# A first quarter of w_in on the plain queue, and batch 0's attention in another order

## The chip, the cores and the metric

The kernel runs on one core of a Trainium2 chip, in one launch. The metric is the device time of that launch in microseconds (us), taken as the median of several runs; the page and the answers of the trace come from one profiled execution. Engines are named as in the profile: PE (TensorE), PEld (its weight loads), DVE (VectorE), ACT (ScalarE), POOL (GpSimd), SP (SyncE). A q behind a name means the engine's instruction queue. DMAs are issued by SP, ACT or POOL.

## The reference

Two stages, each of which takes the whole of the one before. q, k and v are [8 batches, 8 heads, 576 positions, 64] in float32.

```python
scores = scale * q @ k.T                       # per batch and head
rel = pos[:, None] - pos[None, :]
mask = (rel >= 0) & (rel < 128)                # causal, window of 128
scores = where(mask, scores - slopes[h] * abs(rel), -1e9)
attn = softmax(scores)
x = (attn @ v) as [4608 tokens, 512]
h = x @ w_in                                   # w_in [512, 2048]
out = (h * clip(h + 3, 0, 6) / 6) @ w_out      # w_out [2048, 512]
```

## The kernel before

**Tiles.** Attention goes by pairs of heads: four pairs per batch, 32 in all, numbered g = 4 * batch + pair. In a pair the scores fall into diagonal blocks (four of 128x128 per head, bank scd) and blocks off the diagonal (sco). The second stage goes by nine groups of 512 tokens. An "up" unit (moe_up, L462) makes 128 of the 2048 hidden columns for 512 tokens: four matmuls (L451, one for each 128-row slice of x and w_in, called k slice here), one activation on ACT (L470) and one product on DVE (L471) into gbuf. A "down" unit (moe_down, L488) runs four matmuls (L501) of a quarter of w_out for 128 tokens; after four of them the tokens are written out. For the first token group there are 16 up units: 0 to 3 need the first quarter of w_in, 4 to 7 the second, and so on.

**Order.** All engines run a written order (manual_schedule, L718): each engine takes its instructions as the program issues them and waits only for the data and buffers of each. fill(n) (L523) issues the next n units of one list; an up unit is skipped, and the list stands still, as long as the batches that it needs are not done. ORDER (L513) is the list's mixture of ups (U) and downs (D) for each pair of token groups.

**Batch 0** (first_batch, L558). q and k of a pair come as float32 runs (load_run, four transfers on SP's queue, four on ACT's). prepare (L204) casts them to bf16, transposes (L211) turns them on PE, 18 small transposes for q and 18 for k, and copies them out into qTb and kTb. The ALiBi bias and the mask of batch 0 are added on PE: tables_diag (L266) and tables_off (L299) write a table into the bank before the scores are added, so that one exponential covers both heads; where diag_tabled (L263) is false, each head has its own exponential with a bias, and POOL masks the result with a select (L354). The results of batch 0 lie in the still empty w_out_sb. The order is a chain of rounds: transposes of pair g + 1 stand on PE behind the diagonal scores of pair g. When all four pairs have their exponentials, v's five pieces are cast, and attend (L399) multiplies with v for a whole pair in one double bank of ps_sc; DVE divides by the sums (L412, L413). back (L421) transposes the result on PE into the single bank ps_o, and ACT copies it into xT (L438), which is the x of the second stage; for the last pair ACT and DVE copy a part each (L434, L435).

**Weights.** w_in comes in four quarters of 512 columns (load_w_in, L165), float32 in memory and cast to bf16 by the transfer itself, which POOL issues. The first is issued behind a cast of v, the second (second_w_in, L175) behind a write to w_out_sb that waits for pair 1's values, the third and fourth behind the casts of batch 1's q and k. Those come as eight double loads (load_double, L96) on SP's queue, behind batch 0's v (load_tokens, L108); prepare_double (L223) casts them on POOL, wide_double (L248) turns nine 128x128 blocks on PE and copies them out in one piece. Batch 1's v follows on SP's queue.

**Into the second stage.** up_begin (L455) starts a unit with the k slices that are already there: unit 0 with three slices before pair 3 is back, unit 1 with three behind it. fill(1), the turn of batch 1's k, and fill(2) follow; then second_batch (L620) runs batch 1's scores with three units to each pair.

PSUM has eight banks: ps_sc two double ones (scores, attend, wide_double), ps_h two, ps_av and ps_o one each.

Of the kernel before, what the change touches and what calls it, by code (L numbers as in the profile page):

```python
# [18 lines left out]
def kernel(  # L19
# [88 lines left out]
    def load_tokens(b, nm):  # L108
        t = tokens(b, nm)
        for j in range(NQ):  # L110
            n = min(128, S - j * 128)
            nc.sync.dma_start(out=t[:n, j, :, :],
                              in_=src_of[nm][b, :, ds(j * 128, n), :].rearrange("h p d -> p h d"))
# [90 lines left out]
    def prepare(g, copies):  # L204
        for nm, copy in zip("qk", copies):
# [5 lines left out]
    def transposes(g, copies):  # L211
        b, hp = divmod(g, NP)
        for nm, dst, copy in (("q", qTb[b % 2], copies[0]), ("k", kTb[b % 2], copies[1])):
            src = st.pop((g, nm))
            tp = ps_h.tile([128, RT, RP], BF16, tag="h", name="tp", padded_shape=[128, 16, 64])
            for t in range(RT):
                for e in range(2):
                    r = slice(e * D, (e + 1) * D)
                    nc.tensor.transpose(tp[r, t, :], src[r, ts(t, D)], ident[r, r])
            copy(out=dst[:, hp, :, :].rearrange("p j c -> p (j c)")[:, 0:S].rearrange(  # L220
                "p (a t) -> p a t", t=RT), in_=tp.rearrange("p t a -> p a t"))
# [11 lines left out]

    BANKS = {"h": ps_h, "av": ps_av, "o": ps_o}
# [28 lines left out]
    def diag_tabled(g):  # L263
        return g < NP
# [109 lines left out]
    def av_matmuls(g, qts, where):  # L374
# [3 lines left out]
        for qt in qts:  # L378
            for e in range(2):
# [14 lines left out]
    def values(g, qts):  # L394
# [3 lines left out]
        if qts[0] == 0:  # L398
# [5 lines left out]
            in1=rc[:, 0:nq, :, :].to_broadcast([128, nq, 2, D]), op=ALU.mult)  # L404

# [107 lines left out]
    ORDER = [("UUDUDUUDUD", "UUDUDUDUD", "UDUDUDD", "UUDDDD"),  # L513
# [44 lines left out]
    def first_batch():  # L558
        prepare(0, (V, A))
# [27 lines left out]
        load_w_in(0)  # L587
        cast_v(0, 2, V)
        cast_v(0, 3, V)
        cast_v(0, 4, P)  # L590
# [24 lines left out]
        done[0] = NP  # L615
        fill(1)
        wide_double(1, 0, "k", A)
        fill(2)
# [99 lines left out]
    with tc.manual_schedule(engines=every):  # L718
# [7 lines left out]
        load_tokens(0, "v")  # L726
        constants()
# [38 lines left out]
```

## Time and profile before

| | us |
|---|---|
| median of 3 runs | 323.79 (322.96 to 326.55) |
| profiled execution, whole | 323.38 |
| its span, first to last instruction | 321.7 |
| busy in the span: PE | 308.1 (96%) |
| ACT | 195.1 (61%) |
| DVE | 172.7 (54%) |
| POOL | 140.7 (44%) |

The granted TensorE clock is 1.00 over the span. The DMA engines move 51.90 MB, 161 GB/s on average; over the first two thirds of the span their mean busy share is 0.9 or more, later 0.1 to 0.3. HBM is read for 36.70 MB.

A row of the profile names the line of the kernel, the engine, the operation, the tile that is written and those that are read, with partitions x elements; then how many there are, how long they are busy in all or on average, and how long the engine stood idle before them and for whom. In the rows in order of time the first two columns are the start from the span's beginning and the length, in us. In the table by stretches each engine has its busy time and, in brackets, its number of instructions; PEclk is the granted clock, the last two columns are the mean busy share of the 16 DMA engines (over 1 where packets of several queues overlap) and the GB/s moved. The busy time of PE is modelled from the starts of its matmuls, so a full PE there need not be at its peak.

### The profile page before, as it was taken

Reading aid. Unit: us, or ns where it says so; the run is one execution under the profiler, and the core shown is the slowest. Engines: PE = TensorE matmul, PEld = TensorE weight load, DVE = VectorE, ACT = ScalarE, POOL = GpSimd, SP = SyncE. Lnnn points to the kernel's source line nnn. Section 1 sums busy time; section 2 is a strip of 40 time slices with the busy share of each in tenths; the row PEclk is TensorE's granted clock in tenths of the full one; section 3 lists DMA queues with packets and bytes.
Section 4 is the critical chain, followed back from the end, with each engine's and each line's share of the span. In section 5 each row is a group of like instructions: output and inputs, shape, how many; then the busy total and the mean of one; then the engine's idle time right before and its main releaser. Section 6 shows DMA issues by size and latency. Waiting matters only on the chain.

```text
span 321.7 us, 7010 instructions
## 1 busy us (share of the span) xinstructions
PE 308.1 (96%) x2699; PEld 166.7 (52%) x2738; DVE 172.7 (54%) x338; ACT 195.1 (61%) x334; POOL 140.7 (44%) x249
## 2 busy tenths in 40 slices
PE   6879999999999999999999999999999999999996
PEld 5465465555555455455677644554554444444443
DVE  6657675554356555555555556555655455455510
ACT  4748976877777766666676657666764344244401
POOL 8456592683494767356745664563331000000000
PEclk9999999999999999999999999999999999999999
DMA  7999999899999999999999999932112200000112
GB/s 277 202 319 225 272 255 208 223 235 204 220 223 184 220 198 201 200 223 205 186 191 191 229 176 201 211 108 86 23 53 64 76 34 35 33 33 33 67 52 79
DMA packets 131425, 51.90 MB, mean 161 GB/s; under 512 B 118976, under 2 KB 123328, under 8 KB 131392
## 3 DMA queue, kind: packets, MB, share of 16 engines
q1 hardware_dynamic: 126160, 45.36, 67.0%
q0 software_dynamic: 4224, 4.19, 8.3%
q10 hardware_dynamic: 1008, 1.90, 1.6%
q8 instruction: 21, 0.34, 0.5%
q14 instruction: 12, 0.10, 0.1%
HBM read 36.70 MB, written 9.44 MB: 143 GB/s over the span
## 4 chain that ended last, share of the span: by engine, by line
PE 82%; DMA 5%; ACT 4%; POOL 4%; issue 2%; DVE 2%; SPq 1%; POOLq 0%
PE ops L501 35%; PE hps L451 35%; DMA ldbuf<-in_q_dram 3%; PE scd L296 2%; DMA qTb<-tbuf 2%; PE av L391 2%; PE av L383 2%; ACT r L470 2%; PE sco L328 1%; PE ops L482 1%; ACT kTb L244 1%; PE tp L254 1%; POOL tbuf L194 1%; ACT gbuf L351 1%; SPq L98 1%
## 5 line engine op out<-in xcount | busy, mean ns | idle before, releaser
L471 DVE SCALAR_TENSOR_TENSOR gbuf<-r,hps 128x512 bf16<-128x512 f32 x144 | 98.7, 687 | 102.5 <-ACT r L470 100.2
L470 ACT ACTIVATE r<-hps,bias 128x512 f32<-128x512 f32 x144 | 98.9, 689 | 89.5 <-PE hps L451 88.2
L451 PE MATMUL hps<-xT,w_in_sb 128*128 128x512 bf16 (+1 forms) x621 | 142.7, 358 | 2.3 <-DMA w_in_sb<-in_moe_w_in_dram 0.9
L501 PE MATMUL ops<-w_out_sb,gbuf 128*128 128x512 bf16 x540 | 134.2, 380 | 2.3 <-issue 1.7
L451 PEld LDWEIGHTS <-w_in_sb 128*128 128x128 bf16 x640 | 58.8, 98 | 54.8 <-DMA w_in_sb<-in_moe_w_in_dram 1.3
L501 PEld LDWEIGHTS <-gbuf 128*128 128x128 bf16 x560 | 52.2, 98 | 57.2
L354 POOL TENSOR_SCALAR_AFFINE_SELECT pd<-pd 128x512 bf16<-128x512 bf16 x48 | 29.6, 631 | 34.5 <-ACT pd L351 34.4
L364 POOL TENSOR_SCALAR_AFFINE_SELECT po<-po 128x512 bf16<-128x512 bf16 x48 | 30.1, 633 | 32.7 <-ACT po L361 32.6
L351 ACT ACTIVATE pd<-scd,bias_d 128x512 bf16<-128x512 f32 x48 | 31.6, 685 | 5.0 <-PE scd L296 3.6
L194 POOL CAST tbuf<-ldbuf 128x512 bf16<-128x512 f32 (+1 forms) x45 | 25.5, 611 | 18.7 <-DMA qTb<-tbuf 9.8
L510 DVE COPY osb<-ops 128x512 f32<-128x512 f32 x33 | 22.7, 687 | 20.3 <-PE ops L501 20.3
L361 ACT ACTIVATE po<-sco,bias_o 128x512 bf16<-128x512 f32 x48 | 33.1, 689 | 0.0
L402 DVE TENSOR_TENSOR avs<-av,rc 128x384 bf16<-128x384 f32 (+1 forms) x48 | 23.6, 491 | 1.6
L391 PEld LDWEIGHTS <-pd 128*128 128x128 bf16 x192 | 14.4, 97 | 8.3 <-issue 0.5
L383 PE MATMUL av<-vbuf,po 128*128 128x65 bf16 x192 | 18.1, 193 | 0.1
L391 PE MATMUL av<-vbuf,pd 128*128 128x65 bf16 x192 | 17.5, 194 | 0.3 <-ACT kTb L244 0.3
L383 PEld LDWEIGHTS <-po 128*128 128x128 bf16 x192 | 14.4, 98 | 3.1 <-DVE avs L402 0.5
L187 POOL CAST vbuf<-ldbuf 128x1024 bf16<-128x1024 f32 x14 | 14.3, 1040 | 3.2 <-DMA ldbuf<-in_v_dram 3.2
L367 ACT ACTIVATE p4buf<-sco,bias_d 128x64 bf16<-128x64 f32 x48 | 15.5, 324 | 0.0
L227 POOL CAST pr<-ldbuf 128x576 bf16<-128x576 f32 x20 | 12.8, 669 | 4.4 <-DMA ldbuf<-in_k_dram 3.4
L296 PE MATMUL scd<-qTb,kTb 64*128 64x128 bf16 x256 | 12.7, 219 | 1.8 <-DVE kTb L220 1.1
L296 PEld LDWEIGHTS <-kTb 64*128 64x128 bf16 x256 | 7.2, 94 | 13.5 <-issue 9.7
(96 smaller groups left out, 215.0 us busy)
## 6 DMA issues: line engine op xcount, KB each, us to landing
out_dram<-osb SPq DMA_DIRECT2D x33, 256.0 KB, 2.4
ldbuf<-in_v_dram SPq DMA_DIRECT2D x32, 256.0 KB, 5.3
ldbuf<-in_q_dram SPq DMA_DIRECT2D x20, 256.0 KB, 5.1
ldbuf<-in_k_dram SPq DMA_DIRECT2D x16, 256.0 KB, 4.6
ldbuf<-in_q_dram SPq DMA_DIRECT2D x12, 288.0 KB, 6.4
ldbuf<-in_k_dram SPq DMA_DIRECT2D x12, 288.0 KB, 6.4
w_in_sb<-in_moe_w_in_dram POOLq DMA_DIRECT2D x4, 512.0 KB, 9.2
w_out_sb<-in_moe_w_out_dram POOLq DMA_DIRECT2D x4, 512.0 KB, 11.1
```

The source lines that it names most:

```text
L194: nc.gpsimd.tensor_copy(out=tbuf[:m, :, j, :], in_=s[:m, j, :, :].rearrange("p (i e) d -> p i (e d)", e=2))
L296: nc.tensor.matmul(scd[:, e, ts(j, 128)], lhsT=kT[r, j, :], rhs=qT[r, j, :], start=first, stop=first or j == 3)
L351: nc.scalar.activation(out=pd[:, e, :, :].rearrange("p j c -> p (j c)"), in_=sc[:, e, :], func=ACT.Exp, bias=bias_d[:, h:h + 1], scale=scale)
L354: nc.gpsimd.affine_select(out=pd[:, e, :, :], in_=pd[:, e, :, :], pattern=[[0, 4], [1, 128]], channel_multiplier=-1, base=0, compare_op=AL ...
L361: nc.scalar.activation(out=po[:, e, :, :].rearrange("p j c -> p (j c)"), in_=sc[:, e, :], func=ACT.Exp, bias=bias_o[:, h:h + 1], scale=scale)
L364: nc.gpsimd.affine_select(out=po[:, e, :, :], in_=po[:, e, :, :], pattern=[[0, 4], [-1, 128]], channel_multiplier=1, base=-1, compare_op=A ...
L383: nc.tensor.matmul(out_av, lhsT=po[:, e, qt % 4, :], rhs=vb[:, qt - 1, h, :], start=True, stop=False)
L391: nc.tensor.matmul(out_av, lhsT=d, rhs=vb[:, qt, h, :], start=(qt == 0), stop=True)
L451: nc.tensor.matmul(hps[:, lo:hi], lhsT=w_in_sb[:, ks, ts(ms, 128)], rhs=xT[:, ks, ds(src, hi - lo)], start=(ks == 0), stop=(ks == n_ks - 1))
L470: nc.scalar.activation(out=r6, in_=hps, func=ACT.Relu, bias=bias3[:, 0:1], scale=1.0 / 6.0)
L471: nc.vector.scalar_tensor_tensor(out=gts[nt][:, ms, :], in0=r6, scalar=1.0, in1=hps, op0=ALU.min, op1=ALU.mult)
L501: nc.tensor.matmul(ops[nt, sub], lhsT=gts[nt][:, ms, ts(sub, 128)], rhs=w_out_sb[:, ms, :], start=(ms == 0), stop=(ms == n_ms - 1))
```

## The change

- load_raw brings the first quarter of w_in as plain float32 on SP's queue, behind v and ahead of the double loads, into the upper half of gbuf[0], which is not yet in use. cast_raw casts it slice by slice: slices 0 and 1 on ACT behind back(0), slices 2 and 3 on POOL. load_w_in(0) is gone. second_w_in stands behind these casts and those of batch 1's k.
- v's last piece (64 positions) is loaded first. Three pieces are cast on POOL, two on DVE.
- Batch 0's transposes run one pair ahead of its scores and use the banks of ps_o and ps_av in turn with those of ps_h; prepare and transposes take q and k singly. The ten matmuls of the second warm_up are gone.
- Pair 1 is no longer tabled on its diagonal: two exponentials with a bias and two selects on POOL.
- Pair 0's values go by heads (attend_split), in the banks of ps_av and ps_o, ahead of pair 3's scores off the diagonal.
- up_begin(0, 0) takes two slices instead of three. Four units instead of three are issued before batch 1's scores; the turns of batch 1's first k and q both stand among them, and the engines that copy them out change places.
- ORDER for the second token group: one up moves from the last part to the first, ahead of the fourth down.
- attend stands twice in the file, with equal text; the later one is used.

```diff
     def load_tokens(b, nm):
         t = tokens(b, nm)
-        for j in range(NQ):
+        for j in (4, 0, 1, 2, 3) if b == 0 else range(NQ):
...
+    raw = gbuf[0][:, n_ms // 2:n_ms, :].rearrange("p m c -> p (m c)").bitcast(FP32).rearrange(
+        "p (k f) -> p k f", k=n_ks)
+
+    def load_raw():
+        nc.sync.dma_start(out=raw, in_=moe_w_in[:, 0:512].rearrange("(k p) f -> p k f", p=128))
+
+    def cast_raw(ks, copy):
+        copy(out=w_in_sb[:, ks, 0:512], in_=raw[:, ks, :])
...
     def diag_tabled(g):
-        return g < NP
+        return g in (0, 2, 3)
...
-    def av_matmuls(g, qts, where):
+    def av_matmuls(g, qts, where, es=(0, 1)):
...
+    def attend_split(g, tags):
+        avs = st[g, "avs"] = small.tile([128, NQ, 2, D], BF16, tag="avs", name="avs")
+        for e, tag in enumerate(tags):
+            av = BANKS[tag].tile([128, NQ, W], FP32, tag=tag, name="ave",
+                                 padded_shape=[128, NQ, 102])
+            av_matmuls(g, range(NQ), lambda qt, e: av[:, qt, :], (e,))
+            rc = small.tile([128, NQ, 1], FP32, tag="rcs", name="rcs")
+            nc.vector.reciprocal(rc, av[:, :, D:W])
+            nc.vector.tensor_tensor(out=avs[:, :, e, :], in0=av[:, :, 0:D],
+                                    in1=rc.to_broadcast([128, NQ, D]), op=ALU.mult)
...
-    ORDER = [("UUDUDUUDUD", "UUDUDUDUD", "UDUDUDD", "UUDDDD"),
+    ORDER = [("UUDUDUUDUUD","UUDUDUDUD","UDUDUDD","UDDDD"),
...
     def first_batch():
-        prepare(0, (V, A))
+        prepare(0, "qk", (V, A))
         warm_up(20)
         tables_diag(0)
         tables_off(0)
-        warm_up(10)
-        transposes(0, (V, A))
+        transposes(0, "q", "h", V)
+        transposes(0, "k", "h", A)
+        prepare(1, "qk", (P, V))
+        transposes(1, "q", "o", V)
         scores_diag(0)
-        prepare(1, (P, V))
-        transposes(1, (V, V))
+        transposes(1, "k", "av", V)
         scores_off(0)
         exp_full(0)
+        prepare(2, "qk", (P, V))
+        prepare(3, "qk", (P, V))
         scores_diag(1)
-        prepare(2, (P, P))
-        tables_off(1)
-        transposes(2, (V, V))
+        transposes(2, "q", "h", V)
+        transposes(2, "k", "h", V)
+        exp_diag(1, 0)
+        exp_diag(1, 1)
         scores_off(1)
-        exp_full(1)
-        scores_diag(2)
-        prepare(3, (P, V))
-        tables_off(2)
-        transposes(3, (V, V))
-        scores_off(2)
+        transposes(3, "q", "o", V)
+        transposes(3, "k", "av", V)
+        exp_off_full(1)
+        scores(2)
         exp_full(2)
-        scores_diag(3)
-        scores_off(3)
-        exp_full(3)
-        cast_v(0, 0, V)
-        cast_v(0, 1, P)
-        load_w_in(0)
-        cast_v(0, 2, V)
-        cast_v(0, 3, V)
-        cast_v(0, 4, P)
+        for j in (4, 0, 1):
+            cast_v(0, j, P)
+        for j in (2, 3):
+            cast_v(0, j, V)
         for dp in range(2):
             for nm in "kq":
                 load_double(1, dp, nm, nc.sync)
         load_tokens(1, "v")
-        attend(0)
+        scores_diag(3)
+        exp_diag(3, 0)
+        tables_off(3)
+        attend_split(0, ("av", "o"))
+        scores_off(3)
+        exp_off_full(3)
         attend(1)
         back(0)
         attend(2)
+        for ks in (0, 1):
+            cast_raw(ks, A)
         back(1)
+        attend(3)
+        for ks in (2, 3):
+            cast_raw(ks, P)
+        prepare_double(1, 0, (P,), "k")
         second_w_in()
-        prepare_double(1, 0, (P, P))
-        attend(3)
+        prepare_double(1, 0, (P,), "q")
         back(2)
-        up_begin(0, 0, 3)
+        up_begin(0, 0, 2)
         back(3)
-        wide_double(1, 0, "q", V)
         prepare_double(1, 1, (P,), "k")
         load_w_in(2)
         prepare_double(1, 1, (P,), "q")
...
                 load_double(2, dp, nm, nc.sync)
         up_begin(0, 1, 3)
         done[0] = NP
+        fill(2)
+        wide_double(1, 0, "k", V)
         fill(1)
-        wide_double(1, 0, "k", A)
-        fill(2)
+        wide_double(1, 0, "q", A)
+        fill(1)
 
     def second_batch():
         for g in range(NP, 2 * NP - 1):
...
             load_run(g, "k", nc.scalar)
             load_run(g, "q", nc.sync)
         load_tokens(0, "v")
+        load_raw()
         constants()
         memsets()
         memsets_later()
```

More of the change, by code (lines that the diff above doesn't have):

```diff
@@ L202, with prepare @@
     st = {}
-    def prepare(g, copies):
-        for nm, copy in zip("qk", copies):
+    def prepare(g, nms, copies):
+        for nm, copy in zip(nms, copies):
             pr = prs.tile([128, RT * D], BF16, tag=f"pr{nm}", name="pr",
@@ L209, in prepare, with transposes @@
             st[g, nm] = pr
-    def transposes(g, copies):
+    BANKS = {"h": ps_h, "av": ps_av, "o": ps_o}
+    def transposes(g, nm, tag, copy):
         b, hp = divmod(g, NP)
[L213 to L221, printed above, removed]
+        src = st.pop((g, nm))
+        tp = BANKS[tag].tile([128, RT, RP], BF16, tag=tag, name="tp", padded_shape=[128, 16, 64])
+        for t in range(RT):
+            for e in range(2):
+                r = slice(e * D, (e + 1) * D)
+                nc.tensor.transpose(tp[r, t, :], src[r, ts(t, D)], ident[r, r])
+        dst = (qTb if nm == "q" else kTb)[b % 2]
+        copy(out=dst[:, hp, :, :].rearrange("p j c -> p (j c)")[:, 0:S].rearrange(
+            "p (a t) -> p a t", t=RT), in_=tp.rearrange("p t a -> p a t"))
     def prepare_double(b, dp, copies, nms="kq", early=None):
@@ L232, in prepare_double @@
             st[b, dp, nm] = pr
-    BANKS = {"h": ps_h, "av": ps_av, "o": ps_o}
     def double(b, dp, nm, part, tag, copy):
@@ L378, in av_matmuls @@
         for qt in qts:
-            for e in range(2):
+            for e in es:
                 h = 2 * hp + e
@@ L404, in values, with attend @@
             in1=rc[:, 0:nq, :, :].to_broadcast([128, nq, 2, D]), op=ALU.mult)
+    def attend(g):
+        wide = ps_sc.tile([128, 2, 512], FP32, tag="sc", name="wide")
+        av = wide[:, :, 0:NQ * W].rearrange("p e (j c) -> p e j c", j=NQ)
+        av_matmuls(g, range(NQ), lambda qt, e: av[:, e, qt, :])
+        avs = st[g, "avs"] = small.tile([128, NQ, 2, D], BF16, tag="avs", name="avs")
+        rc = small.tile([128, 2, NQ, 1], FP32, tag="rcw", name="rcw")
+        nc.vector.reciprocal(rc, av[:, :, :, D:W])
+        nc.vector.tensor_tensor(out=avs.rearrange("p j e d -> p e j d"), in0=av[:, :, :, 0:D],
+                                in1=rc.to_broadcast([128, 2, NQ, D]), op=ALU.mult)
+    def attend_split(g, tags):
+        avs = st[g, "avs"] = small.tile([128, NQ, 2, D], BF16, tag="avs", name="avs")
+        for e, tag in enumerate(tags):
[6 more added lines that the diff above has]
+                                    in1=rc.to_broadcast([128, NQ, D]), op=ALU.mult)
     def attend(g):
```

## The prediction

> **What bounds the kernel now.** I read the busy time by stretches first, then the stretch that is not full in order of time, then the waits and single transfers in it.
>
> ```profile
> core 0: us, PE busy (x) PEld busy (x) DVE busy (x) ACT busy (x) POOL busy (x), PEclk, DMA share, GB/s
> ...
> 16.00:20.00 4.00, 3.11 (x75) 2.69 (x74) 2.48 (x7) 2.27 (x3) 2.12 (x4) 1.00 1.14 290
> 20.00:24.00 4.00, 2.68 (x44) 2.09 (x43) 2.12 (x4) 1.65 (x3) 2.00 (x3) 1.00 1.09 348
> 24.00:28.00 4.00, 3.95 (x41) 2.37 (x40) 2.63 (x4) 2.88 (x5) 2.60 (x4) 1.00 1.21 252
> 28.00:36.00 8.00, 7.84 (x75) 4.00 (x76) 6.49 (x9) 7.76 (x12) 4.88 (x8) 1.00 1.21 210
> 36.00:50.00 14.00, 13.30 (x173) 8.33 (x175) 9.03 (x16) 12.25 (x20) 11.82 (x19) 1.00 1.12 268
> 50.00:322.00 272.00, 264.79 (x2047) 138.62 (x2077) 139.62 (x261) 159.07 (x284) 107.30 (x187) 1.00 0.72 144
> ```
>
> From 24 us on PE is full (264.79 of 272 us after 50). So the change can win only by starting the full stretch earlier, and in the 14.00 - 13.30 = 0.7 us that PE still idles from 36 to 50. The DMA share is near or over 1 throughout.
>
> The start of the full stretch, in order of time:
>
> ```profile
> 16.61 1.02 ACT L335 ACTIVATE w_out_sb<-sco 128x1024 bf16<-128x1024 f32 x1
> ...
> 22.14 0.33 PEld L451 LDWEIGHTS <-w_in_sb 128*128 128x128 bf16 x3 [0.88 <-DMA w_in_sb<-in_moe_w_in_dram]
> ...
> 23.28 0.37 ACT L434 COPY xT<-tb 128x256 bf16<-128x256 bf16 x1 [1.17 <-PE tb L432]
> 23.69 0.33 DVE L435 COPY xT<-tb 128x320 bf16<-128x320 bf16 x1 [1.67 <-ACT xT L434]
> ...
> 28.39 0.55 PEld L451 LDWEIGHTS <-w_in_sb 128*128 128x128 bf16 x4 [0.39 <-DMA w_in_sb<-in_moe_w_in_dram]
> ```
>
> Batch 0's last exponential ends at 17.63; PE waits 0.88 for the first quarter of w_in; xT of batch 0 is complete at 24.02. The last line is the one that I weigh most: the weights of unit 4, first of the second quarter, come at 28.39, just when PE wants them. Single transfers of w_in, in order, in us from issue to landing:
>
> ```profile
> w_in_sb<-in_moe_w_in_dram POOLq DMA_DIRECT2D x1, 512.0 KB, 9.7
> w_in_sb<-in_moe_w_in_dram POOLq DMA_DIRECT2D x1, 512.0 KB, 10.4
> w_in_sb<-in_moe_w_in_dram POOLq DMA_DIRECT2D x1, 512.0 KB, 6.5
> ```
>
> Issued at 12.38, 17.97 and 26.41, they land at 22.1, 28.35 and 32.94. The packets of each start only when the one before has landed: net 6.2 and 4.6 us for the second and third.
>
> **Batch 0, worked through.** (Durations are the rows of before; about 0.05 from one engine to the next.)
> - Transposes ahead. Pair 1's q transposes now stand on PE before pair 0's diagonal scores. They wait for POOL's cast of q, which ends at 7.48 (6.51 + 0.97, behind the memsets). So these scores move from 6.81 to about 7.9 and their exponential from 7.25 to 8.35: 1.1 us worse. Behind that, the round of before (k copy, scores, tables, transposes, two DVE copies of 0.75) repeated every 2.86 us (scores at 9.53, 12.39, 15.25); its two DVE copies now run beside PE. DVE's casts and copies end at 13.7 instead of 15.2.
> - Pair 1 untabled: PE loses two table matmuls (0.61 together at 8.55), ACT does 1.28 for two halves (row at 27.85) instead of 1.02, POOL gets two selects (0.65 each) while it idles (1.69 before 11.82).
> - ACT: 8.35 + 1.02 x 2 + 1.28 + 1.02 x 5 = 16.8 without gaps. I count 0.7 for pair 2's scores, which stand behind pair 3's transposes, and 0.7 for pair 3's off-diagonal ones, which now stand behind pair 0's values: 18.2, against 17.63.
> - Those values wait for v. Its last piece landed at 15.74; the same bytes in another order end no earlier. DVE's cast (0.42) makes it 16.2, the values 16.7, the off-diagonal scores (0.46) 17.2, their exponential 18.2.
> - Pair 0 by halves: 128x320 was not run; its ends are 128x256 (0.43) and 128x384 (0.56), I take 0.49; reciprocals of 4 and 6 columns cost 0.18 and 0.19. Twice 0.72 against 0.22 + 0.82 is 0.4 more on DVE, but it ends at 17.85 instead of 18.57, as it needs neither the last exponential nor its bank.
> - Then DVE finishes pairs 1, 2, 3 at 18.95, 20.05, 21.2 (before 19.57, 20.76, 22.02). ACT copies pair 0 at 18.25 to 18.9, casts two slices of w_in (673 ns for 576 columns, so 0.6 for 512) to 20.15, copies pair 1 to 20.85 and pair 2 to 22.05. All three copies share one bank, so pair 3's transposes follow at 22.1, and xT is complete at 23.35. **Term 1: 24.02 - 23.35 = 0.67 earlier.** Without the two casts on ACT it would be 1.2 more.
>
> **The weights.** The raw quarter is 1.05 MB on SP's queue behind v and ahead of all four double loads. At the 370 GB/s of 18 to 22 us it takes 2.8 us. v's packets thin out at 14; the next load of SP's queue begins at 14.5 (k, issued 12.31): so raw lands near 18, bounds 17.3 (no gap) and 19.1 (at the pace at which k and q came by 21.8, less the cast transfer's share). ACT wants it at 18.9, so the nearer bound costs nothing and the farther one 0.2; if it came later, the copies of pairs 1 and 2 would wait behind ACT's casts, and k's casts and the second quarter behind POOL's. The double loads lose 2.8 us to it and gain the same from the cast transfer that is gone.
> [...]
> On POOL the second quarter now stands behind two raw casts (0.62 each, from 18.0), and behind k's two casts (0.67 each; its loads land near 18.8 and 19.5): issue at 20.6 instead of 17.97. That costs little, as before it sat until 22.1 behind the first. From issue to landing, a fresh transfer took 9.7 (w_in) and 6.8 (w_out, issued 40.67 on an empty queue): 27.4 to 30.3. The situation is nearest to w_out's, with heavier traffic beside it: I take 7.4, that is 28.0. PE wants it at 23.35 + (28.39 - 24.02) = 27.7. **Term 2: 28.39 - 28.0 = 0.4 of the 0.67 is carried on.** The third and fourth quarters then land near 32.6 and 37.4; units 8 and 12, one slot earlier in the order, want them at 33.3 and 39.
> POOL's chain: what queues behind the second quarter is q's casts, then pair 2 and 3's; w_in's third follows about 2 us earlier than 26.41.
>
> **Three units ahead.** Batch 1's k copy goes to DVE (1.36) and q's to ACT (1.11), the reverse of before, and one unit more runs before batch 1's scores. Unit count is fixed: of four fills between batch 1's attends the last finds no unit. At 42.88 to 49.3 DVE is full with four gbuf products (0.68) and four attends (1.04); one product fewer there. PE can't gain more than its 0.7 idle. **Term 3: 0.3**, bounds 0 and 0.7. ORDER puts the down step that needs w_out's last quarter one unit later: it landed at 57.80 for a use at 58.7, so that covers the earlier front. The order of v's pieces, the ten dropped warm-up matmuls (cover: PE waits for POOL's cast anyway; without it rival 4) and a second, equal attend: nothing.
>
> **Sum.** 0.4 + 0.3 = 0.7 us off the profiled execution's 323.38 (span 321.7 and 1.7 around it); the median 323.79 lies 0.4 above it, so 323.1.
>
> **Rivals.**
> 1. Slower: the second quarter, now first on its queue, inherits the first's slow start. The quarter of before gave 3 to 40 packets per half microsecond from 13.5 to 16, and its last engines dragged from 18.5 to 22.1. At 9.7 it lands at 30.3: unit 4 stalls 2.6, and the two quarters behind land at 35 and 39.8, 1.5 past unit 8's want. Against: traffic then was v's small packets. Loss 30.3 - 28.4 = 1.9, less term 3: 325.4. It decides from a landing past 28.7.
> 2. It does not do what it says: v's landing at 15.7 holds pair 0's values, and the scores behind them, so long that xT is complete at 24 as before. 323.8.
> 3. Faster: ACT's two gap terms (1.4) do not occur and w_in comes at 27.4, so term 1 is 1.7, carried 1.0 to unit 4, all 0.7 of PE's idle time is won: 322.1; with the weights no longer gating, 1.7 + 0.7: 321.4.
> 4. PE's rate. The first 20 warm-up matmuls took 2.31 us, the later ten 0.72: about 0.11 against 0.06 each. With those ten gone and PE idle from 6.05 to 7.53, it could drop to the slow rate: transposes, scores (0.76 + 0.40 + 0.46) of two pairs double, 3.2 us, less 0.7: 326.3. Against: the granted clock reads 1.00 in every stretch, also from 20 to 24 with PE at 2.68 of 4.
> [...]
>
> **How the numbers follow.** Forecast 0.52; rival 1 0.21; rival 2 0.11; rival 3 0.11; rival 4 0.05. The range leaves out the fast end of rival 3, rival 4 and the late end of rival 1: 321.2 to 325.4. One per cent is 3.2 us, about what a measurement of this kernel can tell from no change (its runs span 322.96 to 326.55). Faster by that would need xT complete at 21 and no weight waited for: 0.07. Slower by that: rival 4 past two pairs, and rival 1 with all three quarters late: 0.08. Within: 0.85.
>
> **What would show it.** Right: xT's last copy ends at 23.0 to 23.7; the ACT casts start when pair 0's copy ends, without a DMA wait; unit 4's weight load names w_in's DMA with a short wait, at 27.7 to 28.4; the first exponential starts near 8.3, the last ends near 18.2. Wrong: unit 4 past 29 (rival 1); pair 0's reciprocals past 17.3 (2); exponentials without gaps (3); transposes spaced twice as wide (4); a DMA wait before ACT's casts; a new PE wait for POOL.

## The result, and the profile after

| | before | after |
|---|---|---|
| median of the runs beside each other, us | 323.70 (322.90 to 326.55, 20 runs) | 326.38 (325.26 to 328.62, 20 runs) |
| ratio, 95% interval | | 1.0085 [1.0069, 1.0101] |
| profiled execution, whole / span | 323.38 / 321.7 | 325.26 / 323.5 |

The changed kernel is 2.7 us slower: within one per cent, but well resolved, above the forecast of 323.1 and above the upper end of its range, 325.4. The twenty runs fall into two halves, ten from 325.26 to 326.15 and ten from 326.61 to 328.62, and the median lies between them. The stretches of the changed kernel, with the same columns as before:

```profile
core 0: us, PE busy (x) PEld busy (x) DVE busy (x) ACT busy (x) POOL busy (x), PEclk, DMA share, GB/s
16.00:20.00 4.00, 3.58 (x75) 2.70 (x74) 1.95 (x7) 3.20 (x5) 1.17 (x2) 1.00 1.05 394
20.00:24.00 4.00, 2.89 (x52) 2.34 (x50) 2.51 (x5) 2.94 (x6) 3.76 (x7) 1.00 1.06 380
24.00:28.00 4.00, 3.98 (x32) 2.17 (x30) 2.54 (x4) 2.86 (x5) 3.55 (x6) 1.00 1.30 222
28.00:36.00 8.00, 6.67 (x66) 3.84 (x67) 5.77 (x8) 6.62 (x11) 1.85 (x4) 1.00 1.22 207
...
50.00:322.00 272.00, 266.51 (x2069) 140.18 (x2101) 140.61 (x264) 161.17 (x287) 107.48 (x188) 1.00 0.71 144
```

The hole is between 28 and 36: PE is busy for 6.67 of 8, where it had 7.84; behind 50 it is as full as before. In order of time, the rows of the changed kernel that answer to those of before (start, length, what):

```profile
18.43 1.17 POOL L177 CAST w_in_sb<-gbuf 128x512 bf16<-128x512 f32 x2 [4.00 <-DMA gbuf<-in_moe_w_in_dram]
...
18.69 1.02 ACT L344 ACTIVATE w_out_sb<-sco 128x1024 bf16<-128x1024 f32 x1 [0.45 <-PE sco L337]
...
20.24 1.33 POOL L238 CAST pr<-ldbuf 128x576 bf16<-128x576 f32 x2 [0.64 <-DMA ldbuf<-in_k_dram]
...
20.50 1.14 ACT L177 CAST w_in_sb<-gbuf 128x512 bf16<-128x512 f32 x2
...
21.55 0.88 POOL L166 DMA_DIRECT2D w_in_sb<-in_moe_w_in_dram  x1
...
24.28 0.32 DVE L465 COPY xT<-tb 128x320 bf16<-128x320 bf16 x1 [1.51 <-ACT xT L464]
...
30.09 1.41 PEld L481 LDWEIGHTS <-w_in_sb 128*128 128x128 bf16 x8 [0.88 <-DMA w_in_sb<-in_moe_w_in_dram]
...
30.32 1.67 PE L481 MATMUL hps<-xT,w_in_sb 128*128 128x512 bf16 x7 [0.94 <-DMA w_in_sb<-in_moe_w_in_dram]
```

Three things are seen. The last exponential ends at 19.71, not at 18.2, and xT is complete at 24.60, later than the 24.02 of before. The raw quarter came when ACT wanted it (no wait ahead of ACT's casts). The second quarter is issued at 21.55, behind POOL's raw casts and k's casts, lands at 30.05, and PE waits for it at unit 4: the weight loads stood idle for 0.88 ahead of 30.09 and the matmuls for 0.94 ahead of 30.32, over much the same time. Single transfers of the three quarters that still come by cast transfer, in order, in us from issue to landing:

```profile
w_in_sb<-in_moe_w_in_dram POOLq DMA_DIRECT2D x1, 512.0 KB, 8.5
w_in_sb<-in_moe_w_in_dram POOLq DMA_DIRECT2D x1, 512.0 KB, 8.5
w_in_sb<-in_moe_w_in_dram POOLq DMA_DIRECT2D x1, 512.0 KB, 10.1
```

What the DMA queues moved in two stretches of the changed kernel, first 24 to 25.6, then 26 to 27.5 (packets, MB, share of the 16 engines' time; q1 is SP's queue, q0 the one of POOL's cast transfers):

```profile
q1 hardware_dynamic: 1403, 0.37, 131.8%
q0 software_dynamic: 9, 0.01, 3.4%
...
q0 software_dynamic: 277, 0.28, 114.7%
q1 hardware_dynamic: 73, 0.02, 7.1%
```

The second quarter, issued at 21.55, had hardly begun by 25.6: until then SP's queue filled the engines. Its first packet in the trace starts at 25.46.

Why the exponentials end late is read from batch 0's transposes. Changed kernel, PE:

```profile
5.38 1.17 PE L229 MATMUL tp<-ident,pr 64*64 64x64 bf16 x36
...
10.46 1.17 PE L229 MATMUL tp<-ident,pr 64*64 64x64 bf16 x36
```

and one stretch of it, in the columns of the table by stretches:

```profile
10.86:14.27 3.41, 3.41 (x81) 2.56 (x76) 1.94 (x4) 2.01 (x3) 2.78 (x5) 1.00 1.27 203
```

Before:

```profile
5.32 0.76 PE L219 MATMUL tp<-ident,pr 64*64 64x64 bf16 x36
```

36 transposes take 1.17 instead of 0.76: PE runs at the low rate. The trace's clock records say since when: in this execution the full clock is on record only from 14.27 us, before from 4.07. The PEclk column reads 1.00 all the same, in the stretch shown too: it averages what is on record, and nothing is on record before the first full window. So a PEclk of 1.00 near the start proves nothing; the length of a row that occurs in both kernels does. The mean clock of a run has the same gap. It counts the stretches of 3.41 us at half the clock that come later (0.50 in a_warm below), each of which takes 0.005 off a mean over some 323 us (3.41 x 0.5 / 323: 0.995 for one, 0.989 for two), but not a late start: the profiled execution has a mean of 1.000.

### The profile page after: what moved, and what is told of

Same layout as the page of the kernel before. It is cut to its first block, busy times and chain, and to the rows that moved or that the text cites. A ratio compares the mean times of both kernels' runs of the same rounds, so it can differ in the third digit from the quotient of the medians.

```text
span 323.5 us, 7001 instructions
## 1 busy us (share of the span) xinstructions
PE 310.5 (96%) x2687; PEld 168.8 (52%) x2726; DVE 173.5 (54%) x340; ACT 196.6 (61%) x337; POOL 141.3 (44%) x252
## 4 chain that ended last, share of the span: by engine, by line
PE 83%; DMA 6%; ACT 3%; DVE 2%; issue 2%; SPq 2%; POOL 0%; ACTq 0%; POOLq 0%; DVEq 0%
PE ops L531 36%; PE hps L481 35%; DMA ldbuf<-in_k_dram 4%; DMA w_in_sb<-in_moe_w_in_dram 3%; PE scd L305 2%; PE av L400 2%; PE av L392 2%; PE sco L337 2%; ACT r L500 1%; SPq L112 1%; DVE gbuf L501 1%; PE ops L512 1%; SPq L174 1%; PE tp L251 1%; ACT gbuf L360 1%
## 5 line engine op out<-in xcount | busy, mean ns | idle before, releaser
L501 DVE SCALAR_TENSOR_TENSOR gbuf<-r,hps 128x512 bf16<-128x512 f32 x144 | 98.7, 687 | 103.4 <-ACT r L500 101.4
```

What stands on the lines that cost most here:

```text
L501: nc.vector.scalar_tensor_tensor(out=gts[nt][:, ms, :], in0=r6, scalar=1.0, in1=hps, op0=ALU.min, op1=ALU.mult)
```

## The experiments

Two causes stood against each other at first: the second quarter that comes late (the prediction's rival 1), and PE's low rate (its rival 4, put down there to the ten dropped warm-up matmuls). Later the fills joined them. The times of all kernels, each beside runs of the kernel before on the same chip:

| kernel | median, us | ratio to before, interval |
|---|---|---|
| a_warm | 325.78 | 1.0079 [1.0058, 1.0101] |
| a_w2early | 323.64 | 1.0023 [1.0009, 1.0038] |
| a_warm_w2early | 325.16 | 1.0056 [1.0036, 1.0076] |
| b_nowarm | 322.82 | 0.9994 [0.9981, 1.0007] |
| a_w2_fills | 323.28 | 0.9997 [0.9978, 1.0016] |
| a_noraw | 324.41 | 1.0042 [1.0010, 1.0073] |
| b_raw | 323.21 | 1.0000 [0.9981, 1.0018] |
| a_w2_fills_w8 | 324.25 | 1.0025 [1.0007, 1.0044] |
| b_fills4 | 324.50 | 1.0037 [1.0018, 1.0056] |
| b_raw_late | 325.17 | 1.0057 [1.0039, 1.0074] |
| b_raw_nowarm | 322.93 | 0.9988 [0.9977, 1.0000] |
| a_w2_fills_wide | 323.35 | 0.9999 [0.9989, 1.0010] |
| b_raw_nowarm_e | 326.19 | 1.0086 [1.0069, 1.0103] |
| a_w2_fills_wide_e | 324.12 | 1.0023 [1.0013, 1.0033] |

Kernels whose names begin with a are the changed kernel with an edit, those with b the kernel before with an edit.

### Warm-up or second quarter

**a_warm**, the changed kernel with the second warm-up back:

```diff
         tables_off(0)
+        warm_up(10)
         transposes(0, "q", "h", V)
```

> The changed kernel with the ten warm-up matmuls put back in front of batch 0's transposes. Clock theory (without them PE ran at half rate until 14.27 us): the granted clock is full from about 4.1 us, 36 transposes take 0.76 us instead of 1.17, the last exponential of batch 0 ends near 18.7 instead of 19.7, xT is complete near 23.7 instead of 24.6, and the time falls by 0.9 us or more, its spread of 3.4 us with it. Weights theory (the second quarter of w_in, issued at 21.55 behind POOL's casts, is what PE waits for): the front is earlier as above, but unit 4 still gets its weights at about 30, so the time moves by less than 0.5 us.

**a_w2early**, the second quarter issued ahead of POOL's raw casts:

```diff
         attend(3)
+        second_w_in()
         for ks in (2, 3):
             cast_raw(ks, P)
         prepare_double(1, 0, (P,), "k")
-        second_w_in()
```

> The changed kernel with the second quarter of w_in issued on POOL ahead of its two raw casts and of k's casts (fence and transfer as they were). Weights theory: issued near 19.2 instead of 21.55, landed near 28 instead of 30.05, unit 4 starts without a DMA wait near 29.3 instead of 30.3, the time falls by about 1 us. Clock theory: no more than 0.3 us, since the front itself is late.

**a_warm_w2early**, both:

> Both edits. If both causes are real they add up only together: xT complete near 23.7, unit 4 near 28.3, as in the kernel before; the time is within 0.5 us of the kernel before (323.7), some 2.7 us under the changed kernel. If a third cause (one unit more ahead of batch 1's scores) weighs too, it stays 0.5 to 1 us above.

**b_nowarm**, the kernel before without its second warm-up:

```diff
         tables_off(0)
-        warm_up(10)
```

> The kernel before without the ten warm-up matmuls and with nothing else changed. Clock theory: the granted clock is full only from about 7.5 us or later, the rounds of batch 0's transposes take 0.4 us longer each until then, the time rises by 0.5 to 2 us. Rival (those ten are filler in a wait; the rate comes from the order of the transposes): no change within 0.3 us.

The warm-up gains nothing: 1.0079 with it against 1.0085 in the changed kernel, 0.9994 without it in the order of before. The early second quarter takes 0.0062 of the 0.0085 away, 2.0 us. Its profile is also the first in which the changed order ran at the full clock from 5.33 on: the last exponential ends at 18.19 and xT is complete at 23.08, as the prediction had worked out (18.2, 23.35).

Both edits together did not come within 0.5 us of before, as was expected: 325.16 in five runs, 1.5 us above the 323.64 of the early second quarter alone. In the profile of both, PE is at half the clock from 14.63 to 18.04, pair 1's values come late, and the second quarter, which waits for them, is issued at 20.09 instead of 17.93 and lands near 29.3. So there the ten matmuls cost rather than help. Whether they bring such a fall on is not shown: nine of the twelve runs without them have a mean clock of 0.988 to 0.995 too.

In both profiles with the warm-up back the full clock is on record early (from 5.91 and 4.39), but it did not last. The changed kernel with the warm-up back, in stretches of 3.41 us between which its clock changes:

```profile
9.32:12.74 3.42, 3.34 (x97) 2.25 (x98) 3.42 (x6) 2.94 (x4) 2.85 (x5) 1.00 1.38 214
12.74:16.15 3.41, 1.66 (x23) 0.92 (x22) 1.31 (x3) 1.48 (x2) 0.88 (x2) 1.00 1.01 219
16.15:19.56 3.41, 3.41 (x45) 2.47 (x45) 1.05 (x4) 1.57 (x3) 1.17 (x2) 0.50 1.05 398
19.56:22.98 3.42, 2.83 (x69) 2.55 (x67) 2.89 (x7) 3.13 (x5) 2.59 (x5) 1.00 1.06 396
```

PE was busy for 1.66 of 3.41 in one stretch, and the next was granted half the clock. Part of that idle time has no releaser. Same kernel, PE:

```profile
14.26 0.38 PE L305 MATMUL scd<-qTb,kTb 64*128 64x128 bf16 x7 [1.55 <-issue]
```

### Fills, order, raw quarter, code

**a_w2_fills**, a_w2early with three units ahead and the ORDER of before:

```diff
-        fill(2)
+        fill(1)
         wide_double(1, 0, "k", V)
...
-    ORDER = [("UUDUDUUDUUD","UUDUDUDUD","UDUDUDD","UDDDD"),
+    ORDER = [("UUDUDUUDUD", "UUDUDUDUD", "UDUDUDD", "UUDDDD"),
```

> The changed kernel with the second quarter of w_in issued ahead of POOL's raw casts (323.64 in the first group), and now three units ahead of batch 1's scores and the ORDER of before. Theory: the fourth unit ahead is what loses the 1.1 us between products no. 15 and 16 (they stood 5.58 us apart with four units ahead, 4.36 apart before); with three the two stand about 4.4 apart, the last written tile starts at 317.4 to 317.8 instead of 318.61 and the time is about 322.6. Rival: those four units only bring work forward, the loss is in batch 1's attends themselves (their exponentials or v's casts are late), and the time stays at 323.6. My prediction's term 3 would have three units 0.3 slower: 323.9.

**a_noraw**, the changed kernel with both quarters by the cast transfer: the new order of batch 0 without the raw quarter, the second quarter ahead of k's casts, the four units ahead kept:

```diff
-        load_raw()
...
-        for j in (4, 0, 1):
-            cast_v(0, j, P)
+        for j in (4, 0):
+            cast_v(0, j, P)
+        load_w_in(0)
+        cast_v(0, 1, P)
...
-        for ks in (0, 1):
-            cast_raw(ks, A)
         back(1)
         attend(3)
-        for ks in (2, 3):
-            cast_raw(ks, P)
+        second_w_in()
         prepare_double(1, 0, (P,), "k")
-        second_w_in()
```

> The changed kernel without the raw quarter: w_in's first quarter comes by the cast transfer again, issued behind the second of POOL's casts of v, the second quarter behind pair 1's values as before, no casts of w_in on ACT and POOL. So the new order of batch 0 alone, with four units ahead. Theory: the order itself brings the clock's half-rate windows; the last exponential ends at 18.2 where the clock is full and near 20 where it is not, most runs show a clock of 0.995 or less, and with a first quarter that lands 9 us after its issue at 13.7 (22.7) unit 0 waits: 324.5 to 325.5. Rival: the raw transfer in the traffic brings them; then nearly all runs show a clock of 0.998 or more, as before.

**b_raw**, the kernel before with load_raw and cast_raw of the change:

```diff
-        load_w_in(0)
...
         attend(2)
+        for ks in (0, 1):
+            cast_raw(ks, A)
         back(1)
         second_w_in()
+        for ks in (2, 3):
+            cast_raw(ks, P)
         prepare_double(1, 0, (P, P))
```

> The kernel before with the raw quarter alone: plain transfer on SP's queue behind v, two slices cast on ACT behind pair 0's copy and two on POOL behind the second quarter's issue; order of batch 0, fills and ORDER as before. Theory: the clock stays full; the raw quarter lands near 18.4, PE's wait of 0.88 for the first quarter at 22.14 goes, two casts on ACT (1.2) delay the copies into xT by about as much, the second quarter is issued at about 18 and lands near 28.1 as in the run with it early: 322.6 to 323.6. Rival: if the plain transfer itself costs (double loads later, batch 1's casts later), 324 or more.

**a_w2_fills_w8**, a_w2_fills with warm_up(8) for warm_up(20):

> As the first kernel of this group, with eight warm-up matmuls instead of twenty at the start. PE stood still, waiting for nothing that the trace shows, always at its 449th instruction: until 14.26, 14.26 and 13.97 in three profiles, 1.4 to 1.6 us after a 16 KB packet of the instruction queue (12.71, 12.85, 12.35); before reached that instruction at 13.63, when the packet had long landed (11.74). Theory: it is the loading of code; 24 instructions fewer put the place where PE stands still 24 instructions later in the program, into the diagonal scores of pair 3, where PE waits for a bank anyway; PE then has a fuller window of 3.41 us there, the runs with a clock of 0.995 become rare, and the time is 0 to 0.7 below the first kernel's. Rival: the stop stays at the same place of the program, or the clock drops as often; no difference. If the clock rises later for want of warm-up matmuls, over 1 slower.

a_w2_fills: products no. 15 and 16 (of the second stage, on DVE) stand 4.36 apart again, as before; with four units ahead they stood 5.58 apart in all profiles of the change. The medians give 0.0026 for that, 0.8 us, so the theory holds in direction and is short of the 1.1 expected. The two intervals overlap, and its profile had the full clock only from 14.02, so this size is rough.

a_noraw and b_raw separate the order from the raw quarter. The order without it ran with a mean clock of 0.983 to 0.990 in six of twelve runs (two or more half-rate stretches each), and in the profile at full clock only from 14.18. The raw quarter in the order of before ran at 0.998 to 1.0 in all twelve and costs nothing, nor does it gain. The falls of the clock in these two kernels go with the order of batch 0, not with the raw quarter.

The theory of a_w2_fills_w8 failed: 324.25, one microsecond worse than a_w2_fills. Its profile has the full clock only from 15.13, while eleven of its twelve runs show a mean clock of 0.999 or 1.0; so a late start is the likely cause, and the mean does not show it. PE did not stand still at its 449th instruction, but with the full clock only from 15.13 it reached that only near 17, so this run does not test the theory that it is the loading of code.

### The same costs in the steady order, and a front without clock trouble

**b_fills4**, the kernel before with four units ahead, the turns and the ORDER of the change:

```diff
         back(3)
-        wide_double(1, 0, "q", V)
...
-        fill(1)
-        wide_double(1, 0, "k", A)
-        fill(2)
+        fill(2)
+        wide_double(1, 0, "k", V)
+        fill(1)
+        wide_double(1, 0, "q", A)
+        fill(1)
```

> The kernel before with the fills, the turns of batch 1's first q and k and the ORDER of the changed kernel, nothing else: four units ahead of batch 1's scores in a kernel whose clock is steady. Theory: products no. 15 and 16 stand about 5.6 us apart instead of 4.36, the last written tile starts about 1.1 later and the time is 324.1 to 324.5 where before has 323.2. Rival: the gap of 5.58 belongs to the changed front (late exponentials of batch 1), and here the two stand 4.4 apart; the time is 322.9 to 323.3 (term 3 of the prediction: 0.3 less).

**b_raw_late**, b_raw with the second quarter behind POOL's casts:

```diff
-        second_w_in()
         for ks in (2, 3):
             cast_raw(ks, P)
-        prepare_double(1, 0, (P, P))
+        prepare_double(1, 0, (P,), "k")
+        second_w_in()
+        prepare_double(1, 0, (P,), "q")
```

> The kernel before with the raw quarter, and the second quarter issued behind POOL's two raw casts and the two casts of batch 1's k, as in the change. Against the run with the raw quarter and the second quarter ahead of these casts (323.21, landing 28.26). Theory: issue moves to about 21 to 21.6, the landing to 29.5 to 30.2, unit 4 waits 1.3 to 2 us more and the time is 324.6 to 325.2. Rival: with the steady clock the transfer on an empty queue needs only 7 us, lands before 28.7 and costs nothing: 323.2 to 323.6.

**b_raw_nowarm**, b_raw without the second warm-up:

> The kernel before with the raw quarter and without the second ten warm-up matmuls: the two parts of the change that cost nothing in this order. Theory: raw alone had the last tile start 0.45 earlier, without the warm-up the exponentials end 0.24 earlier: 322.6 to 323.0, the lowest of all kernels, at or just below before. Rival: unit 4's weights gate (landing near 28.2 in both) and nothing is gained over the raw quarter alone: 323.2.

**a_w2_fills_wide**, a_w2_fills with other warm-up matmuls:

```diff
+    def warm_wide(n):
+        w = ps_av.tile([128, 4, 128], FP32, tag="av", name="ww")
+        for _ in range(n):
+            nc.tensor.matmul(w, lhsT=ident,
+                             rhs=ident.rearrange("p (o c) -> p o c", o=1).to_broadcast([128, 4, 128]),
+                             start=True, stop=True)
...
-        warm_up(20)
+        warm_wide(5)
         tables_diag(0)
         tables_off(0)
+        warm_wide(3)
```

> The changed kernel with the second quarter early and three units ahead (323.28, its clock full only from 14.02 in the profile and one or two windows short in a third of its runs), with the twenty warm-up matmuls of 128 columns replaced by five of 512, and three more of 512 ahead of batch 0's first transposes: 24 instructions fewer, more columns. Theory: the clock rises in the first or second window (4 to 8 us) because PE is fuller there, PE does not stand still at its 449th instruction because that is now pair 3's scores, where it waits for a bank anyway; most runs show 0.998 or more, the last exponential ends near 18.2, xT is complete near 23.1, and the median is 322.6 to 322.9. Rival: the order with its waits for POOL and ACT leaves windows short whatever stands ahead of them: 323.2 to 323.6, with clocks down to 0.989 as before.

b_fills4 settles the fills, with the turns and the ORDER that go with them: 324.50 against 323.23, 1.3 us slower, at a clock of 0.999 or 1.0 in every run, with the same 5.58 (47.42 to 53.00). How it comes about, PE in the kernel with four units ahead:

```profile
27.97 0.66 PE L254 MATMUL tp<-ident,pr 128*128 128x128 bf16 x9 [0.42 <-ACT qTb L256]
...
47.56 0.45 PE L432 MATMUL tb<-ident,avs 128*128 128x128 bf16 x5 [0.58 <-DVE avs L413]
...
49.15 0.45 PE L432 MATMUL tb<-ident,avs 128*128 128x128 bf16 x5 [0.30 <-DVE avs L413]
```

The last fill between batch 1's attends has no unit left, so PE has nothing between two attends of DVE (1.04 each) and waits 0.58 and 0.30 for them, where before it waited 0.19 and 0.21 about there. From 24 to 28 PE is busy for 3.41 against 3.95: the changed turns of q and k put ACT's copy of q ahead of the next transposes, the wait in the first row. So this part is the turns', not the fourth unit's. From 36 to 50 PE is busy for 13.00 against 13.30. The two parts together, 0.8, are what the two profiled executions differ by (324.17 and 323.38); the medians lie further apart.

b_raw_late settles the second quarter. It is issued at 21.72 and lands at 30.48:

```profile
30.52 0.55 PEld L460 LDWEIGHTS <-w_in_sb 128*128 128x128 bf16 x4 [2.15 <-DMA w_in_sb<-in_moe_w_in_dram]
```

and in b_raw, issued at 17.69:

```profile
28.30 0.55 PEld L460 LDWEIGHTS <-w_in_sb 128*128 128x128 bf16 x4 [0.72 <-DMA w_in_sb<-in_moe_w_in_dram]
```

325.17 against 323.21: 2.0 us, with nothing changed but the order of POOL's work, and with the full clock from 5.52 and 4.29 in the two profiles.

a_w2_fills_wide has the clock full from 6.72 in its profile and a mean clock of 0.998 or more in all twelve runs, which lie within 0.72 us. The last exponential ends at 18.23, xT is complete at 23.12: the front as worked out, 0.9 us earlier than before. The time does not follow: 323.35, the same as before. The rival's times came, but not for its reason. PE now waits for the weights:

```profile
28.65 0.55 PEld L488 LDWEIGHTS <-w_in_sb 128*128 128x128 bf16 x4 [1.08 <-DMA w_in_sb<-in_moe_w_in_dram]
```

b_raw_nowarm, 322.93, has the lowest ratio of all, with an interval that just reaches 1; it is not shown to be faster than before.

### Can the second quarter come earlier?

Issued between 17.7 and 18.6, it landed between 28.1 and 28.6 in all seven profiles, whatever else was changed. Two runs issue it with the casts of v, without the write that waits for pair 1's values:

```diff
         cast_v(0, 1, P)
+        load_w_in(1)
...
-        second_w_in()
```

> The run with the raw quarter and without the second warm-up (322.93), and the second quarter issued where the first's cast transfer stood, behind POOL's first cast of v near 12.4, with no wait for pair 1's values. Theory 1, the issue decides: the second quarter lands near 22 to 24, unit 4 does not wait, the third and fourth come earlier too, and the time is 322.0 to 322.6. Theory 2, the traffic decides: the DMA engines are full from 12 to 28, so what it gains the raw quarter, v or batch 1's loads lose: raw lands 1 to 3 us later than 18.4, ACT's casts wait for it and with them the copies into xT, and the time is 323.2 to 324.5.

> The run with the changed order at full clock and three units ahead (323.35, xT complete at 23.12, unit 4 waiting 1.08 for a landing at 28.61), and the second quarter issued behind POOL's casts of v, near 14.5 instead of 17.97. Theory 1, the issue decides: landing at 24 to 26, no wait at unit 4, the earlier xT is carried on and the time is 322.3 to 322.8. Theory 2, the traffic decides: raw lands later than 18.3 by about a microsecond or more, the casts on ACT wait, and nothing is gained: 323.2 to 324.

It lands at 23.04 and 24.52, and both kernels are slower than without the edit, by 3.3 us and 0.8 us. The issue does move the landing, as theory 1 has it, but the time goes with the other loads, as theory 2 has it. In the first, the raw quarter goes from 18.43 to 20.43 and ACT waits for it:

```profile
20.45 1.14 ACT L177 CAST w_in_sb<-gbuf 128x512 bf16<-128x512 f32 x2 [0.75 <-DMA gbuf<-in_moe_w_in_dram]
...
25.53 1.14 PE L263 MATMUL tp<-ident,pr 128*128 128x128 bf16 x9 [1.54 <-POOL pr L236]
```

The second row is the price behind it: batch 1's k, cast late, keeps PE waiting, and 1.14 for nine transposes that otherwise take 0.68 shows the low rate once more (here a fall in the order of before). The stretches of 3.41 us, same kernel:

```profile
18.05:21.47 3.42, 2.25 (x55) 2.06 (x52) 3.12 (x7) 1.66 (x3) 0.99 (x2) 1.00 1.11 297
21.47:24.88 3.41, 1.53 (x13) 0.83 (x12) 0.71 (x2) 1.67 (x4) 2.25 (x5) 1.00 1.05 400
24.88:28.29 3.41, 2.76 (x15) 1.66 (x16) 1.36 (x1) 0.00 (x0) 3.24 (x6) 0.50 1.10 277
```

PE is busy for 1.53 of 3.41, and half the clock follows; the mean clock of all five runs is 0.994 or 0.995, so a part of the 3.3 us is the clock's. The DMA share is over 1 throughout. In a_w2_fills_wide_e the raw quarter still lands at 18.43, but PE waits 1.7 for the cast of batch 1's data at 25.86 instead of 1.08 for weights. In both tries, what unit 4 no longer waits for is lost again, and more, at loads that PE needs before 28.

## Why the prediction was wrong

What bounded the kernel was read rightly (unit 4's weights, full DMA engines, a full PE behind). Going through the steps:

- **Transposes ahead, exponentials at 18.2, term 1.** Right where the clock is full: first exponential at 8.08 to 8.61, last end at 18.19 to 18.23, xT complete at 23.08 to 23.12, in three profiles. That is 0.9 before the 24.02 of before; term 1 had 0.67. In the profile on record the clock was not full, and 19.71 and 24.60 came of it.
- **The raw quarter** landed at 18.38 (forecast near 18), the plain transfer costs and gains nothing (b_raw 1.0000), and ACT's casts did not wait. Right.
- **Term 2: the second quarter at 28.0.** This is the step that failed most: it landed at 30.05, and that is worth 2.0 us, measured twice (a_w2early against the changed kernel; b_raw_late against b_raw). About half is the issue, put at 20.6 and come at 21.55: raw landed 0.4 late, and k's loads landed at 20.09 and 20.85 where 18.8 and 19.5 were taken, since all double loads stand behind the raw quarter on SP's queue; that they gain back what they lose to it, as the sum had it, was the author's estimate, and no run shows it. The rest is the time from issue to landing, taken as 7.4, near w_out's 6.8, and measured at 8.5. From the first packet to the landing the two took the same, 4.6 and 4.7; but w_out's first packet came 2.1 after its issue (40.67 to 42.76), the second quarter's 3.9 after (21.55 to 25.46). The prediction also reckoned that a later issue costs little, since before the transfer sat until 22.1 behind the first quarter. In b_raw nothing stands ahead of it on its queue, it is issued at 17.69, and it still takes 10.6 to land, against 10.4 in before; the DMA share there is 1.03 from 17.94 to 21.36. In the changed kernel SP's queue took 117.1% of the 16 engines' time from 21.55 to 25.45. What exactly holds the first packet back is not shown.
- **Rival 1** had the right delay, and its landing at 30.3 is nearly exact, but that is partly luck: its issue was 0.95 too early and its 9.7 from issue to landing 1.2 too long. The start was late rather than slow: no packet before 25.46, then 92 per half microsecond (277 of q0 from 26 to 27.5), where it feared 3 to 40.
- **Term 3: 0.3 gained by four units ahead.** Wrong in sign. The prediction saw that the last fill finds no unit, and counted DVE's relief; it did not ask what PE has to do there, nor what the turns of q and k do to PE. Taking the fourth unit and its ORDER back gains about 0.8 (a_w2_fills against a_w2early); unit, turns and ORDER together cost 1.3 us in the order of before (b_fills4). With rival 1's loss of 1.9 and 0.8 lost here, the sum is 323.7 + 1.9 + 0.8 = 326.4; by this sum it is the sign of term 3 that takes the time past the range.
- **"Dropped warm-up: nothing".** Right: in none of the three pairs of kernels is the one with the ten matmuls clearly faster.
- **Rival 4, PE's rate,** came about, with the wrong cause: the ten dropped matmuls do not decide it, and in the profile on record the rate did not drop but never rose before 14.27. That its 326.3 is so near the measured 326.38 is luck, as the loss lies in terms 2 and 3. It was given 0.05 because the granted clock read 1.00 in every stretch. That column shows a later fall (0.50 in a_warm), but nothing ahead of the first full stretch. What goes with the falls is the order of batch 0 (a_noraw: 0.983 to 0.990 in six of twelve runs), in which PE waits for POOL's cast (0.68 ahead of 7.22 in the changed kernel); and in the two profiles with the warm-up back, the stretch ahead of the fall holds a stop of 1.55 and 1.62 that has no releaser. Why the clock rose late in the profile on record stays open: its first stretch of 3.41, with 2.60 us of PE busy, began at 0.62, and no full clock followed until 14.27; that of before, with 2.64, began at 0.66, and the full clock followed at 4.07.

The range has a slip: its lower end, 321.2, takes in the 321.4 that it is said to leave out. Nothing hangs on it.

By parts, in ratios: the late second quarter 0.0062, the fills 0.0026, the rest -0.0003, together 0.0085. In the steady order the first two measured 0.0057 and 0.0037. These are differences of medians over runs whose clocks differ, so what the clock alone costs is not separated. The front's gain of 0.9 us is real, but no time is left of it: in the profile on record, with the full clock only from 14.27, xT is complete 0.6 later than before, and with the clock full from 6.72 the second quarter lands at 28.6, when PE has waited 1.08 for it (a_w2_fills_wide).

## What to carry to other kernels

With a DMA share of 1.05 to 1.30 from 16 to 36, as in the changed kernel, moving a transfer to another queue gained nothing here (b_raw, 1.0000), and issuing one earlier only chose which load was late (b_raw_nowarm_e: the second quarter at 23.04, the raw one at 20.43 instead of 18.43, the time 3.3 us up). So list every transfer that the busy engine needs by a given time, and price a new one by rows from the same stretch of traffic, the time to its first packet apart from the packets. A unit of work that covers a gap can be moved ahead only once; look at what the engine does in the gap that it leaves. And judge the clock at the start by the length of a row that both kernels have, not by a mean clock.

## What the runs showed of the hardware

- **The granted clock changed in steps of 3.41 us, which begin at another time in each profile.** In twelve of the sixteen profiles it is full from a time between 4.07 and 6.72, in four, all of the changed order, only from 14.02 to 15.13. In a_warm it is full from 5.91 to 16.15, three times 3.41, and half from there to 19.56. Half the clock (0.50) followed stretches in which PE was busy for 1.53 (b_raw_nowarm_e), 1.66 (a_warm) and 1.79 (a_warm_w2early) of 3.41 us. No threshold follows, as one stretch with 1.55 (a_noraw, 21.01 to 24.42) was not followed by a fall.
- **With a few wide matmuls in place of many narrow ones, no fall of the clock was on record.** With five of 512 columns and three more in place of twenty of 128 (a_w2_fills_wide), no run of twelve has a mean clock under 0.998, against five of twelve at 0.989 to 0.995 (a_w2_fills). A late start would not show in these means, but the two profiles with wide matmuls are full from 6.72 and 5.21, and the twelve times lie within 0.72 us, against 1.35. Which of the two, width or the added three, went with it was not tried apart. In no profile of the order of before does the first stretch begin ahead of 0.66 us, so whether its clock would be late there too stays open.
- **PE stood still at the same count of its instructions in three profiles.** All three are of the changed order (a_warm, a_warm_w2early, a_w2early): it waited, with no releaser, at its 449th recorded instruction: to 14.26, 14.26 and 13.97, for 1.55, 1.62 and 0.69. In one of them the program has ten matmuls and ten weight loads less ahead (a_w2early), and the place moved with the count. A 16 KB packet of the instruction queue had ended 1.4 to 1.6 before (12.71, 12.85, 12.35). Before reached that instruction at 13.63, with the packet in at 11.74, and did not wait. That PE waited there for the loading of code was the author's estimate; no run shows it. a_w2_fills_wide, with the place moved on by 24 instructions, had no such wait.
- **Two cast transfers stood for 2.1 and 3.9 us before their first packet.** The first packet of w_out's came 2.1 us after its issue in before (40.67 to 42.76), that of the second quarter 3.9 in the changed kernel (21.55 to 25.46); SP's queue took 103.4% and 117.1% of the 16 engines' time meanwhile. In b_raw the second quarter, with nothing ahead of it on its queue, landed 10.6 after its issue at 17.69.
